# Scaling a head's exponentials on three engines instead of one, in a fused attention and mixture kernel

## The chip, the cores and the metric

The kernel runs on one core of one Trainium2 chip. The time is that of one execution on the device, in microseconds (us). Engines are called as the profile calls them: PE is TensorE (matmuls; PEld its weight loads), DVE is VectorE, ACT is ScalarE, POOL is GpSimd, SP is SyncE.

## What is computed

Causal attention with a decay for 4 batches of 8 heads, 576 tokens of 64 values, and on its output a mixture of four experts:

```python
scores = scale * np.matmul(q, k.transpose(0, 1, 3, 2))
log_f = np.log(np.clip(f, 0.0001, 1.0))
cum = np.cumsum(log_f, axis=-1)
decay = cum[:, :, :, None] - cum[:, :, None, :]
scores = np.where(causal, -1000000000.0, scores + decay)
scores = scores - np.max(scores, axis=-1, keepdims=True)
attn = np.exp(scores)
attn = attn / (np.sum(attn, axis=-1, keepdims=True) + 1e-09)
x = np.matmul(attn, v)          # heads side by side: 2304 x 512

p = domain_probs / (domain_probs.sum(-1, keepdims=True) + 1e-09)
for e in range(E):              # E = 4, w1[e] 512 x 1024, w2[e] 1024 x 512
    h = np.maximum(x @ w1[e], 0.0)
    out += p[:, e:e + 1] * (h @ w2[e])
```

The change touches the division of the exponentials by their sum.

## The kernel before

All is float32. A factor of a matmul is split into a high part (a Copy on ACT that rounds) and a low part (a subtraction of the high part), and a product is made of two or three matmuls of such parts.

Attention runs head by head. A batch is cut into two halves of query rows: half 0 has 256 queries in two tiles (t = 0 and 1), half 1 has 320 in three (t = 2, 3 and 4, with 384, 512 and 576 keys). A head of half 1 is called a long head here; there are 32, of which the 24 of batches 1 to 3 are "early", which means that their exponentials are divided before the product with `v`; in the others the product is scaled afterwards. For each tile of a head `qk_pe` (L378) makes the scores `s` in PSUM, `qk_min` (L392, DVE) adds the mask, keeps the negated scores in the SBUF tile `p` and their minimum in `nm`, and `qk_exp` (L407, ACT) turns `p` into exponentials in place and keeps their sum. When all tiles of an early head are done, `norm` adds 1e-9 to the sums (L435, DVE), takes the reciprocal `rs` (L438, DVE) and multiplies each tile of `p` by its column of `rs` (L442): on POOL for a long head, on DVE for a short one. One head later `tr_pe` (L479) transposes the blocks of `p` on PE, `tr_hi` (L489, ACT) and `tr_lo` (L496 and L504, DVE) turn them into `pth` and `ptl`, and `av_pe` (L529) multiplies them with `v` into `o`; `av_top` (L552, ACT) and `av_add` (L565, DVE) take that out of PSUM. Six buffers hold `p`, three of them for each long head.

Before a head is due, `prep` splits its queries and keys: `hi` (L325, ACT), `q` (L326, POOL), `kl` (L334) and the low half of `hi` (L340), the last two on DVE for a long head; `prep_v` does so for `v` (L306, ACT, and L313, DVE).

In between run the steps of the experts, 256 tokens and 256 hidden columns at a time: `l1` (L783), the gate, which makes `gh` (L794, ACT) and `gl` (L795, DVE), `l2` (L813), and the accumulation `acc` (L835, DVE). Their weights come by DMA, are rounded on ACT (`wh`, L750) and split on POOL (`wl`, L755; some of the first on DVE). A third part, after the attention, makes the last tokens' products with fewer matmuls (L953 and L1011); its sums and splits are on POOL too (L895, L910, L933).

The Python order of the attention's steps among the experts' steps follows fixed costs (`head_steps`, `pace`). Within it a planner with a simulated timeline chooses the order of the instructions on each engine; only the start-up (`startup`) has an order written out by hand. PE, ACT, DVE and POOL then each run their own queue in order, held by semaphores. DMAs are issued from SP.

Of the kernel before, what the change touches and what calls it, by code (L numbers as in the profile page):

```python
# [10 lines left out]
AF = mybir.ActivationFunctionType  # L11
ALU = mybir.AluOpType
# [57 lines left out]
def fused(ctx: ExitStack, tc: tile.TileContext, qk, v, f, probs, w, out):  # L70
    nc = tc.nc
# [182 lines left out]
    class Job:  # L254
# [178 lines left out]
        def norm(self, hh):  # L433
            rs = self.rs[:, hh, :]
            nc.vector.tensor_scalar(  # L435
                out=rs, in0=self.ssum[:, hh, :], scalar1=1e-9, scalar2=None, op0=ALU.add
            )
            nc.vector.reciprocal(out=rs, in_=rs)  # L438
            for t in self.its:
                i, x = t - self.its[0], self.p[hh, t][:, : TOK0[t] + 128]  # L440
                eng = nc.gpsimd if self.half else nc.vector
                eng.tensor_scalar(  # L442
                    out=x, in0=x, scalar1=rs[:, i : i + 1], scalar2=None, op0=ALU.mult
                )

        def spread(self):

# [815 lines left out]
```

## Time and profile before

| | us |
|---|---|
| three runs | 975.55, 976.8, 977.25; median 976.8 |
| the profiled execution, whole | 975.0 |
| its span, first to last instruction | 973.2 |

| engine | busy us | share of the span |
|---|---|---|
| PE | 960.6 | 99% |
| DVE | 676.4 | 70% |
| POOL | 513.6 | 53% |
| ACT | 467.2 | 48% |

Busy time is the time in which an engine has an instruction of its own under way; the ends of matmuls are modelled. The list of waits names, for each engine and line, who ended its idle time. The chain that ended last is followed back from the last instruction. The timeline shows each instruction with its start and duration, and several of one kind in a row as one piece.

### The profile page before, as it was taken

The page shows a single profiled execution, that of the slowest core. Times are in us where ns is not written, and L with a number is a line of the kernel's source. Part 1 is how long each engine was busy: PE and PEld are TensorE (multiplying, and loading weights), DVE is VectorE, ACT ScalarE, POOL GpSimd, SP SyncE. Part 2 cuts the span into 40 slices and gives each one's busy share as a digit, 9 for nine tenths or more (in the row PEclk, how much of TensorE's full clock was granted, in tenths as well). Part 3 has the DMA queues.
Part 4 walks back from the last instruction along what each step waited for, and adds up shares of the span by engine and source line. Part 5 has one row for each costly group of instructions (what it writes and reads, how often), then busy time and mean ns, then how long its engine had stood idle before and what let it go on. Part 6 is the DMA issues. An engine that isn't in the chain of part 4 may idle for free.

```text
span 973.2 us, 15567 instructions
## 1 busy us (share of the span) xinstructions
PE 960.6 (99%) x5638; PEld 843.7 (87%) x5638; DVE 676.4 (70%) x1413; ACT 467.2 (48%) x979; POOL 513.6 (53%) x511
## 2 busy tenths in 40 slices
PE   8999999999999999999999999999999999999998
PEld 6898999899899999998999998988788888888886
DVE  6877777877877676778769656357766666566665
ACT  7776664646656455556455544334323232233220
POOL 4988763502306547548457565778654444555410
PEclk9999999999999999999999999999999999999999
DMA  7765431322312312313313030421211112111002
GB/s 257 254 205 169 140 92 42 110 84 95 128 53 89 103 52 96 97 52 117 96 57 134 2 109 22 130 90 63 87 44 43 44 44 73 58 44 43 23 1 87
DMA packets 29822, 85.89 MB, mean 88 GB/s; under 512 B 3160, under 2 KB 5264, under 8 KB 29744
## 3 DMA queue, kind: packets, MB, share of 16 engines
q1 hardware_dynamic: 29744, 84.89, 26.8%
q8 instruction: 45, 0.74, 0.3%
q14 instruction: 33, 0.27, 0.1%
HBM read 80.00 MB, written 4.87 MB: 87 GB/s over the span
## 4 chain that ended last, share of the span: by engine, by line
PE 83%; POOL 5%; DVE 5%; issue 3%; DMA 2%; ACT 1%; SPq 0%; POOLq 0%; DVEq 0%; ACTq 0%
PE l L783 19%; PE l L813 19%; PE y L1011 17%; PE m L953 13%; PE s L378 5%; PE t L479 5%; PE o L529 5%; POOL bwl L933 2%; DMA wr<-in_w 2%; POOL wt L910 1%; POOL wl L755 1%; DVE v L313 1%; DVE kl L334 1%; POOL rx L895 1%; DVE rl L897 1%
## 5 line engine op out<-in xcount | busy, mean ns | idle before, releaser
L783 PE MATMUL l<-xl,wh 128*128 128x256 f32 x640 | 180.8, 283 | 0.3 <-DVE xl L673 0.3
L783 PE MATMUL l<-xh,wh 128*128 128x256 f32 x640 | 180.9, 283 | 0.2 <-ACT xh L672 0.2
L783 PE MATMUL l<-xh,wl 128*128 128x256 f32 x640 | 180.6, 283 | 0.0
L755 POOL TENSOR_TENSOR wl<-wr,wh 128x512 fp32r<-128x512 f32 x114 | 151.9, 1358 | 30.5 <-ACT wh L750 19.2
L835 DVE SCALAR_TENSOR_TENSOR acc<-y,prob,acc 128x512 f32<-128x512 f32 x120 | 88.3, 747 | 68.5 <-PE y L1011 68.5
L442 POOL TENSOR_SCALAR p<-p,rs 128x384 f32<-128x384 f32 (+2 forms) x72 | 107.8, 1513 | 50.1 <-DVE rs L438 46.8
L813 PE MATMUL l<-wh,gh 128*128 128x512 f32 x320 | 127.2, 397 | 0.8 <-DVE acc L835 0.8
L813 PE MATMUL l<-wl,gh 128*128 128x512 f32 x320 | 126.7, 396 | 0.0
L813 PE MATMUL l<-wh,gl 128*128 128x512 f32 x320 | 125.0, 394 | 0.0
L407 ACT ACTIVATE p<-p,nm 128x576 f32<-128x576 f32 (+2 forms) x160 | 95.6, 598 | 58.4 <-DVE nm L392 57.1
L783 PEld LDWEIGHTS l<-xl,wh 128*128 128x128 f32 x640 | 120.5, 188 | 3.3 <-DVE xl L673 0.5
L783 PEld LDWEIGHTS l<-xh,wh 128*128 128x128 f32 x640 | 120.4, 188 | 3.4 <-ACT xh L672 0.4
L933 POOL TENSOR_TENSOR bwl<-wr,bwh 128x256 fp32r<-128x256 f32 (+1 forms) x80 | 78.5, 1008 | 80.0 <-ACT bwh L930 80.0
L783 PEld LDWEIGHTS l<-xh,wl 128*128 128x128 f32 x640 | 120.4, 188 | 0.2
L392 DVE CUSTOM_DVE_ANT_0 p<-s,mask 128x288 f32<-128x288 f32 (+2 forms) x160 | 74.8, 478 | 57.6 <-PE s L378 52.4
L326 POOL CAST q<-raw 64x320 fp32r<-64x320 f32 (+1 forms) x56 | 27.3, 488 | 145.7 <-PE s L378 131.8
L1011 PE MATMUL y<-bwh,hh 128*128 128x512 f32 x256 | 101.2, 395 | 0.8 <-DVE acc L835 0.8
L1011 PE MATMUL y<-bwl,hh 128*128 128x512 f32 x256 | 101.1, 395 | 0.0
L1011 PE MATMUL y<-bwh,hl 128*128 128x512 f32 x256 | 100.4, 395 | 0.0
L953 PE MATMUL m<-rl,bwh 128*128 128x512 f32 x224 | 87.5, 390 | 0.0
L953 PE MATMUL m<-rh,bwh 128*128 128x512 f32 x224 | 87.4, 390 | 0.0
L953 PE MATMUL m<-rh,bwl 128*128 128x512 f32 x224 | 87.0, 392 | 0.0
(121 smaller groups left out, 2097.4 us busy)
## 6 DMA issues: line engine op xcount, KB each, us to landing
wr<-in_w SPq DMA_DIRECT2D x96, 512.0 KB
raw<-in_qk SPq DMA_DIRECT2D x16, 896.0 KB
raw<-in_qk SPq DMA_DIRECT2D x12, 512.0 KB
vr<-in_v SPq DMA_DIRECT2D x16, 320.0 KB
out<-acc SPq DMA_DIRECT2D x16, 256.0 KB
vr<-in_v SPq DMA_DIRECT2D x8, 128.0 KB
first<-in_qk SPq DMA_DIRECT2D x3, 256.0 KB
first<-in_v SPq DMA_DIRECT2D x4, 128.0 KB
```

Source lines behind the costliest of these rows:

```text
L378: nc.tensor.matmul(out=ps[:, at : at + z - a], lhsT=lhsT, rhs=rhs, start=(m == 0), stop=(m == 1),)
L392: nc.vector.tensor_tensor_reduce(out=pt[:, a:z], in0=ps, in1=mask[:, m0 + a : m0 + z], scale=-0.125, scalar=BIG if n == 0 else nm[:, col : ...
L407: return nc.scalar.activation(out=pt[:, :w_], in_=pt[:, :w_], func=AF.Exp, scale=-1.0, bias=self.nmax[hh][:, c : c + 1], accum_out=self.ss ...
L442: eng.tensor_scalar(out=x, in0=x, scalar1=rs[:, i : i + 1], scalar2=None, op0=ALU.mult)
L479: nc.tensor.transpose(ps[:, at : at + 128], self.p[hh, it][:, TOK0[jt] : TOK0[jt] + 128], ident)
L755: eng.tensor_tensor(out=wl[n][:, a:z], in0=wraw[n][:, a:z], in1=wh[n][:, a:z].bitcast(F32), op=ALU.subtract)
L783: nc.tensor.matmul(out=self.l1p[:, fi, :], lhsT=lhsT, rhs=rhs[:, k, :], start=(k == 0 and m == 0), stop=(k == 3 and m == 2),)
L813: nc.tensor.matmul(out=l2[tt], lhsT=lhsT, rhs=rhs, start=(self.ps == 0 and fi == 0 and m == 0), stop=(self.ps == 1 and fi == 1 and m == 2),)
L835: nc.vector.scalar_tensor_tensor(out=acc[c][:, tt, :], in0=ps, scalar=sc, in1=acc[c][:, tt, :], op0=ALU.mult, op1=ALU.add,)
L933: nc.gpsimd.tensor_tensor(out=lo[:, a:z], in0=x[:, a:z], in1=hi[:, a:z].bitcast(F32), op=ALU.subtract)
L953: nc.tensor.matmul(out=ps, lhsT=lhsT[:, o], rhs=rhs[:, k, :], start=(k == 0 and i == 0), stop=(k == 1 and i == 2),)
L1011: nc.tensor.matmul(out=ps, lhsT=lhsT, rhs=rhs, start=(fi == 0 and m == 0), stop=(fi == 1 and m == 2),)
```

## The change

For a long head, tile t = 2 (384 columns) is now scaled by an activation Copy on ACT whose scale is the column of `rs`, tile t = 3 (512 columns) on DVE, and tile t = 4 (576 columns) still on POOL. The short heads' tiles (t = 0 and 1) stay on DVE.

```diff
             for t in self.its:
                 i, x = t - self.its[0], self.p[hh, t][:, : TOK0[t] + 128]
-                eng = nc.gpsimd if self.half else nc.vector
-                eng.tensor_scalar(
-                    out=x, in0=x, scalar1=rs[:, i : i + 1], scalar2=None, op0=ALU.mult
-                )
+                r = rs[:, i : i + 1]
+                if t == 2:
+                    nc.scalar.activation(out=x, in_=x, func=AF.Copy, scale=r)
+                    continue
+                eng = nc.gpsimd if t == 4 else nc.vector
+                eng.tensor_scalar(out=x, in0=x, scalar1=r, scalar2=None, op0=ALU.mult)
```

## Rows read from the trace of the kernel before

**Rows 1.** Busy time by stretch, 290 to 576 us; columns in its first line.

```profile
core 0: us, PE busy (x) PEld busy (x) DVE busy (x) ACT busy (x) POOL busy (x), PEclk, DMA share, GB/s
290.00:576.00 286.00, 285.74 (x1932) 264.25 (x1931) 206.67 (x510) 160.05 (x332) 171.87 (x135) 1.00 0.25 84
```

**Rows 2.** Waits of PE and PEld, 290 to 580: total us, times, longest.

```profile
PE l L813 <- DVE acc L835: 0.3, 1, 0.3
...
PEld o L529 <- DVE ptl L496: 0.8, 3, 0.4
```

**Rows 3.** The page's chain that ended last: by engine, by line.

```profile
PE 83%; POOL 5%; DVE 5%; issue 3%; DMA 2%; ACT 1%; SPq 0%; POOLq 0%; DVEq 0%; ACTq 0%
PE l L783 19%; PE l L813 19%; PE y L1011 17%; PE m L953 13%; PE s L378 5%; PE t L479 5%; PE o L529 5%; POOL bwl L933 2%; DMA wr<-in_w 2%; POOL wt L910 1%; POOL wl L755 1%; DVE v L313 1%; DVE kl L334 1%; POOL rx L895 1%; DVE rl L897 1%
```

**Rows 4.** Timeline of PE: start, duration, what; in brackets idle time and releaser.

```profile
453.20 0.50 PE L813 MATMUL l<-wh,gh 128*128 128x512 f32 x1 [0.26 <-DVE acc L835]
...
596.51 0.50 PE L813 MATMUL l<-wh,gh 128*128 128x512 f32 x1 [0.56 <-DVE acc L835]
...
684.83 0.50 PE L1011 MATMUL y<-bwh,hh 128*128 128x512 f32 x1 [0.77 <-DVE acc L835]
```

**Rows 5.** Groups of L442 by shape, 290 to 580: count, busy us, mean ns.

```profile
L442 POOL TENSOR_SCALAR p<-p,rs 128x576 f32<-128x576 f32 x24 | 41.4, 1724 | 0.0
L442 POOL TENSOR_SCALAR p<-p,rs 128x512 f32<-128x512 f32 x24 | 37.6, 1565 | 0.0
...
L442 POOL TENSOR_SCALAR p<-p,rs 128x384 f32<-128x384 f32 x24 | 30.0, 1249 | 50.1 <-DVE rs L438 46.8 <-ACT pth L489 3.2
```

**Rows 6.** Timeline of POOL and PE, the head at 320 us.

```profile
320.82 4.48 POOL L442 TENSOR_SCALAR p<-p,rs 128x384 f32<-128x384 f32 x3
...
325.61 0.27 PE L479 MATMUL t<-ident,p 128*128 128x128 f32 x1
```

**Rows 7.** Groups of ACT by shape, whole span.

```profile
L591 ACT ACTIVATE xh<-xs 128x256 fp32r<-128x256 f32 x16 | 6.6, 414 | 9.7 <-DVE xs L581 9.7
L896 ACT ACTIVATE rh<-rx 128x512 fp32r<-128x512 f32 x8 | 4.9, 624 | 4.5 <-POOL rx L895 4.5
```

**Rows 8.** Line L442 on DVE, all: least, median, longest ns.

```profile
L442 DVE TENSOR_SCALAR p<-p,rs x32: 271/343/853, 93.0 to 197.1; 128x128 f32<-128x128 f32 x16, 128x256 f32<-128x256 f32 x16
```

**Rows 9.** Timeline of DVE, two short heads' pairs of scalings.

```profile
101.27 0.55 DVE L442 TENSOR_SCALAR p<-p,rs 128x128 f32<-128x128 f32 x2
...
119.02 1.12 DVE L442 TENSOR_SCALAR p<-p,rs 128x128 f32<-128x128 f32 x2
```

**Rows 10.** Timelines of DVE and POOL, at 315, 449 and 488 us.

```profile
314.58 0.74 DVE L334 TENSOR_TENSOR kl<-raw,hi 64x576 fp32r<-64x576 f32 x1
...
315.40 5.44 POOL L755 TENSOR_TENSOR wl<-wr,wh 128x512 fp32r<-128x512 f32 x4 [1.31 <-ACT wh L750]
...
317.12 1.15 DVE L435 TENSOR_SCALAR rs<-ss 128x3 f32<-128x3 f32 x1
...
448.71 2.53 POOL L755 TENSOR_TENSOR wl<-wr,wh 128x512 fp32r<-128x512 f32 x2
...
448.93 2.92 DVE L334 TENSOR_TENSOR kl<-raw,hi 64x576 fp32r<-64x576 f32 x1
...
487.61 0.17 DVE L435 TENSOR_SCALAR rs<-ss 128x3 f32<-128x3 f32 x1
```

**Rows 11.** Timelines of DVE and PE, the heads at 440 and 381 us.

```profile
439.45 0.49 DVE L496 TENSOR_TENSOR ptl<-t,pth 128x320 fp32r<-128x320 f32 x1
...
441.19 0.31 PE L529 MATMUL o<-ptl,v 128*128 128x320 f32 x1
...
381.98 0.49 DVE L496 TENSOR_TENSOR ptl<-t,pth 128x320 fp32r<-128x320 f32 x1
...
382.52 0.41 PE L529 MATMUL o<-ptl,v 128*128 128x320 f32 x1
```

**Rows 12.** Timelines of ACT and DVE, the head at 377 us.

```profile
377.03 0.19 ACT L407 ACTIVATION_READ_ACCUMULATOR p<-p,nm 128x1 f32 x1
...
381.15 0.16 DVE L438 RECIPROCAL rs<-rs 128x3 f32<-128x3 f32 x1
```

## The prediction

> **What bounds the kernel now.** I read the busy time by stage first, then who made TensorE wait, then the chain that ended last, and only then the operations that the change moves. The long heads that the change touches (three query tiles, half 1, batches 1 to 3: 24 heads) run from 290 to 576 us. In this stretch PE is busy for 285.74 of 286.00 us at the full granted clock, 1.00, which is the 2.4 GHz level [rows 1]. Everything else has room: DVE 206.67 us (72%), ACT 160.05 (56%), POOL 171.87 (60%). The list of waits says the same from the other side: in the whole stretch PE's matmuls waited once, 0.3 us, for an accumulation on DVE, and the weight loads 0.8 us in three pieces for `ptl` [rows 2]. The chain that ended last is 83% PE; POOL has 5% of it [rows 3], and the POOL lines that the page names there are the splits and sums of the late stage, not the scalings at L442. So a microsecond taken from POOL in this stretch is not a microsecond of the kernel. What the edit can do to the time is what it does to PE's waits, which are nearly nil.
>
> **How much can be gained at most.** PE's idle gaps from 290 us on, up to its last matmul, are 0.26 us at 453.20, 0.56 at 596.51 and 0.77 at 684.83 [rows 4], 1.59 us in all. A better order cannot take away more than these, and 1.59 us is 0.16% of 976.8. About 0.2%, 1.95 us, is what a measurement of this kernel can tell from no change. I leave the first 290 us out of account: there the heads have two query tiles, and the edit keeps those scalings on DVE.
>
> **The change part by part.** *Removed from POOL:* 24 scalings of 128x384 (30.0 us) and 24 of 128x512 (37.6 us); the 24 of 128x576 (41.4 us) stay [rows 5]. POOL in the stretch goes from 171.87 to 171.87 - 67.6 = 104.3 us, 36%. The three scalings of a head are one run of 4.49 us today; one alone takes 1.72. The last scaled tile is therefore ready some 2.7 us sooner. Who waits for it? The transposes of that head. In the tightest head the POOL run ends at 320.82 + 4.48 = 325.30 and the first transpose starts at 325.61 [rows 6], 0.3 us later; the other 23 have 0.8 to 9 us. No row shows PE waiting for POOL, so the 2.7 us go into slack that exists already: worth 0.
>
> *Added to ACT:* 24 Copies of 128x384, SBUF to SBUF, with a scale from a column. The trace of before has no such instruction at this width. A Copy of 128x256 takes 0.414 us and one of 128x512 0.624 [rows 7]; these are the bounds, and half-way between the widths lies half-way between the times, 0.52. 24 x 0.52 = 12.5 us, ACT goes to 172.5 us, 60%. Copy already runs on ACT in every head beside Exp, and the only table loads of the trace stand at lines 156 and 180 in the start, so none is added. A cost below nothing is excluded: it is work that ACT did not have.
>
> *Added to DVE:* 24 scalings of 128x512. The nearest rows are the same line on DVE in the short heads: a pair of 128x128 and 128x256, 384 columns in two instructions, takes 0.55 us when nothing holds it and 1.12 when something does [rows 9]. One instruction has one fixed start instead of two, so 512 columns lie between 0.34 (the median of all 32 of that line [rows 8]) and 0.55 x 512 / 384 = 0.73; I take 0.5. 24 x 0.5 = 12 us, and DVE goes to 218.7 us, 76%.
>
> What may be added on DVE is waiting for POOL. Undisturbed, the subtraction `kl` takes 0.74 us; begun 0.22 us after two of POOL's splits it took 2.92, and `rs`, one tiny instruction with a single tensor, took 1.15 while POOL split, where 0.17 is usual [rows 10]. Both have SBUF inputs alone. So the moved scaling can be held too, by about 1 us in a typical case (1.15 - 0.17), which makes 1.5 us the upper price of one and 36 us of DVE the upper sum (85% busy). On the other hand POOL's long runs at L442, which hold DVE in their turn, become 2.7 us shorter per head, and the splits behind them may start sooner. I take no net change in the holding and keep both ends for the range.
>
> The Trainium skill speaks against this edit here: "SBUF — State Buffer", section "SBUF: two separate sides", says that VectorE and GpSimd share a port pair which one instruction holds until it is done, for a VectorE operation with two SBUF inputs or in a two-port mode. This trace agrees in kind (2.92 us against 0.74), and even shows a wait over two GpSimd instructions in a row. [...]
>
> *Waits that the change adds.* All three scalings wait for `rs`. On DVE that is the instruction's own engine; queued behind it are the `ptl` subtractions of the head before, and the `o` matmuls wait for those. Their cover is the thinnest of the kernel: usually about a microsecond or more (last `ptl` ends at 439.94, first matmul that reads one starts at 441.19), but 0.05 us in the head at 381 (ends at 382.47, read at 382.52) [rows 11]; three of the 24 heads have under 0.7 us at their last `o` matmuls. An unheld 0.5 us there costs at most 3 x 0.5 = 1.5 us, and nothing where the planner puts it behind them. On ACT, what queues behind the new Copy are `pth` evictions, gates (`gh`) and the next head's exponentials. `rs` ends 0.6 to 3 us after the last exponential in 21 heads and 3.8 to 4.1 in three, of which the worst has 377.22 to 381.31 [rows 12]. Gates have more cover: in the whole stretch PE waits for no `gl` [rows 2]. No DMA is issued by any of the moved instructions, and SP's queue is not touched. The order on each engine comes from the planner, which sees other durations now, so PE's order may be shuffled too; at 100% busy with several microseconds between producer and reader, that has no sign that I can give.
>
> **The sum.** Gain 0 from POOL (at most 1.59 us through other waits), loss 0 to 1.5 us from DVE in front of `ptl`, 0 from ACT. The middle of the loss, about 0.7, against a chance that the wait at 453.20 goes, 0.3, leaves +0.4. The profiled execution took 975.0 us with a span of 973.2; the three timed runs have a median of 976.8, so I add the same sum to that: 977.2, hence a forecast of no measurable change.
>
> **Rivals.** *Slower, DVE held in front of `ptl`.* The mechanism is the wait on POOL above: the moved scaling, released by `rs`, meets POOL's 128x576 scaling, released by the same `rs`, or a split. It decides from the point where 1.5 us of delay exceed the cover of `ptl`. With today's order that is three heads, 3 x 1.2 = 3.6 us: 976.8 + 3.6 = 980.4. For it: three heads are already late for this very reason (`kl` held by splits), and the one wait of a PE matmul in the stretch came out of such a pile [rows 4, 10]. Against it: the scaling follows `rs` on the same engine and POOL needs a hand-over, so DVE should start first and POOL, which has the room, would wait. This rival is what the page of the Trainium skill named above leads one to expect.
>
> *Slower, ACT held.* If the Copy stands in ACT's queue ahead of the `pth` evictions, these start up to 4.1 + 0.5 us late, some 2.5 us more than the usual distance from `pth` to `o`. In the three heads where `rs` is that late: 3 x 2.5 = 7.5, 984.3 us. Against it: those evictions are ready before `rs` is, and the planner queues by readiness.
>
> *Faster.* POOL, relieved, starts its splits sooner, they no longer fall on `kl`, and the DVE piles behind PE's waits vanish: at most 1.59 us, 975.2, which is still inside 0.2%. Only if matmuls also follow each other more closely would it be more, say 974.7.
>
> *The edit does less than it says.* Only `t == 2` and `t == 4` leave DVE, and both occur in long heads alone, so it does what it says; this would end at no change as well.
>
> **How the numbers follow.** No measurable change 0.76 (977.2, from 975.2 to 978.7); DVE held 0.13 (980.4); ACT held 0.04 (984.3); faster 0.07 (974.7). That gives faster 0.07, same 0.76, slower 0.17. The range reaches from 974.6, which takes in the gain, to 980.8, which takes in the DVE rival with 0.4 us to spare; left out are the ACT rival and what lies beyond the worked-out price of the DVE rival.
>
> **What would show it.** In the changed profile: 24 ACT Copies of about 0.52 us, 24 DVE scalings of about 0.5 us (a mean above 0.8 means they are held), 24 POOL scalings of 1.7 us or somewhat more, POOL some 67 us lighter between 290 and 576. PE idle in that stretch should stay under 2 us. I am wrong if PE waits for `ptl` or `pth` in many heads, if PE's idle time outside the stretch changes by microseconds because the planner reorders the late stage, or if the time falls by more than PE's 1.59 us of idle.

## The result, and the profile after

| | kernel before | changed kernel |
|---|---|---|
| median of 4 runs each, side by side, us | 976.95 (975.55 to 977.25) | 982.2 (980.92 to 984.01) |
| ratio, 95% interval | 1 | 1.0055 [1.0037, 1.0073] |
| the profiled execution, us | 975.0 | 982.76 |
| its span, us | 973.2 | 980.9 |

The change makes the kernel slower: by 5.25 us between the medians, and by a ratio of 1.0055, whose interval lies clear of 1. A second set of runs (below, "changed again") gave 1.0047. The forecast was no measurable change, 977.2 us with a range to 980.8, and the measured time lies above that range.

The engines' busy times, from the page of the changed kernel, say that the exchange took place: POOL went from 513.6 to 449.4 us. PE went from 960.6 to 966.5, though it has the same matmuls to do.

```profile
PE 966.5 (99%) x5638; PEld 851.0 (87%) x5638; DVE 691.2 (70%) x1437; ACT 480.2 (49%) x1003; POOL 449.4 (46%) x463
```

The moved scalings themselves, as groups by shape from 290 to 580 us in the changed kernel (count, busy us, mean ns, then idle time before them and who ended it). They answer to [rows 5]: lines 443 and 446 are what line 442 was.

```profile
L446 POOL TENSOR_SCALAR p<-p,rs 128x576 f32<-128x576 f32 x24 | 44.4, 1849 | 79.5 <-DVE rs L438 60.5 <-ACT pth L491 19.1
...
L443 ACT ACTIVATE p<-p,rs 128x384 f32<-128x384 f32 x24 | 14.8, 618 | 17.2 <-DVE rs L438 17.2
...
L446 DVE TENSOR_SCALAR p<-p,rs 128x512 f32<-128x512 f32 x24 | 12.5, 521 | 0.1
```

All three are where the edit puts them, 24 each. Now the stretches, in the busy-time view of the changed kernel (columns in its first line; [rows 1] is the same view of before).

```profile
core 0: us, PE busy (x) PEld busy (x) DVE busy (x) ACT busy (x) POOL busy (x), PEclk, DMA share, GB/s
290.00:574.00 284.00, 284.00 (x1932) 263.92 (x1931) 223.81 (x548) 179.14 (x370) 105.14 (x85) 1.00 0.26 82
574.00:584.00 10.00, 5.83 (x18) 4.29 (x17) 8.66 (x9) 1.14 (x3) 9.23 (x7) 0.67 0.35 113
...
584.00:980.90 396.90, 391.25 (x1812) 322.79 (x1811) 238.49 (x332) 115.59 (x198) 186.47 (x193) 1.00 0.18 56
...
577.50:584.30 6.80, 5.01 (x13) 4.09 (x14) 5.19 (x6) 0.00 (x0) 6.03 (x5) 0.50 0.49 157
```

Where the moved instructions run, among the long heads, PE has not one wait left: 284.00 of 284.00 us. In the ten microseconds after them it is busy for 5.83, and its clock is at 0.50, the 1.2 GHz level, for some 7 us (577.5 to 584.3). The PE timeline of the changed kernel (start, duration, what; in brackets idle time and who ended it) shows the same place; it answers to [rows 4].

```profile
574.13 0.28 PE L785 MATMUL l<-xh,wl 128*128 128x256 f32 x1
576.16 0.47 PE L815 MATMUL l<-wh,gh 128*128 128x512 f32 x1 [1.75 <-DVE acc L837]
...
579.29 0.80 PE L815 MATMUL l<-wh,gh 128*128 128x512 f32 x1 [2.42 <-DVE acc L837]
...
580.30 0.63 PE L815 MATMUL l<-wh,gl 128*128 128x512 f32 x1
580.73 0.63 PE L815 MATMUL l<-wh,gh 128*128 128x512 f32 x1
...
584.35 0.28 PE L785 MATMUL l<-xh,wh 128*128 128x256 f32 x1
...
642.04 0.39 PE L815 MATMUL l<-wh,gl 128*128 128x512 f32 x1
642.27 0.39 PE L955 MATMUL m<-rh,bwh 128*128 128x512 f32 x1
...
692.61 0.50 PE L1013 MATMUL y<-bwh,hh 128*128 128x512 f32 x1 [1.40 <-DVE acc L837]
```

PE waits 1.75 us and then 2.42 us for an accumulation `acc` on DVE. Behind the second wait its matmuls of 512 columns follow each other at 0.43 us (580.30 to 580.73) where later ones do at 0.23 (642.04 to 642.27). Why `acc` is late stands in DVE's and POOL's timelines of the same microseconds. DVE first.

```profile
568.55 6.68 DVE L899 TENSOR_TENSOR rl<-xf,rh 128x512 fp32r<-128x512 f32 x4 [0.82 <-ACT rh L898]
575.26 0.75 DVE L837 SCALAR_TENSOR_TENSOR acc<-l,prob,acc 128x512 f32<-128x512 f32 x1
575.93 2.64 DVE L899 TENSOR_TENSOR rl<-xf,rh 128x512 fp32r<-128x512 f32 x2
578.49 0.74 DVE L837 SCALAR_TENSOR_TENSOR acc<-l,prob,acc 128x512 f32<-128x512 f32 x1
```

POOL in the changed kernel, beside it:

```profile
565.76 5.51 POOL L757 TENSOR_TENSOR wl<-wr,wh 128x512 fp32r<-128x512 f32 x4 [11.04 <-ACT wh L752]
571.23 1.76 POOL L897 TENSOR_TENSOR rx<-xf,xf 128x512 f32<-128x512 f32 x1
573.07 1.61 POOL L897 TENSOR_TENSOR rx<-xf,rx 128x512 f32<-128x512 f32 x1
574.64 6.30 POOL L757 TENSOR_TENSOR wl<-wr,wh 128x512 fp32r<-128x512 f32 x4
```

The `rl` subtractions are the low parts of the last tokens' inputs, the first work of the third part. Four of them stand ahead of the first `acc` in DVE's queue, and POOL splits weights and makes sums from 565.76 on without a pause. The four take 6.68 us, 1.67 each, beside splits and sums alike. The same place in the kernel before, DVE and then POOL:

```profile
589.65 3.56 DVE L897 TENSOR_TENSOR rl<-xf,rh 128x512 fp32r<-128x512 f32 x3 [0.82 <-ACT rh L896]
593.24 0.75 DVE L835 SCALAR_TENSOR_TENSOR acc<-l,prob,acc 128x512 f32<-128x512 f32 x1
593.91 1.88 DVE L897 TENSOR_TENSOR rl<-xf,rh 128x512 fp32r<-128x512 f32 x3
...
596.97 1.28 DVE L897 TENSOR_TENSOR rl<-rx,rh 128x512 fp32r<-128x512 f32 x2
```

```profile
589.05 1.30 POOL L895 TENSOR_TENSOR rx<-xf,xf 128x512 f32<-128x512 f32 x1 [13.58 <-ACT tmp L552]
590.42 1.64 POOL L895 TENSOR_TENSOR rx<-xf,rx 128x512 f32<-128x512 f32 x1
597.80 1.62 POOL L895 TENSOR_TENSOR rx<-rx,xf 128x512 f32<-128x512 f32 x1 [5.74 <-DVE rl L897]
```

There, three `rl` and not four precede the first `acc`; POOL has no split, only two sums, and where it is idle an `rl` takes 0.63 to 0.64 us (1.88 / 3 and 1.28 / 2). PE waited 0.56 us at that place [rows 4].

Why did this block of work meet POOL's splits? It came sooner. Both timelines of ACT, before and after, have as a landmark the last eviction of the attention, which opens the third part:

```profile
587.80 0.43 ACT L552 ACTIVATE tmp<-o 64x320 f32<-64x320 f32 x1 [3.99 <-PE o L529]
```

```profile
566.70 0.43 ACT L554 ACTIVATE tmp<-o 64x320 f32<-64x320 f32 x1
```

It is 21 us earlier. The planner works with the durations of the new scalings, by which a head's scaling is over sooner, and its order brings the attention's last heads forward among the experts' steps: ahead of the attention's last matmul PE does 150 of the experts' matmuls fewer than before. PE's own work does not get shorter by that, it is only done in another order. The first `rl` moves with it, from 589.65 to 568.55, to where POOL has eight splits to do.

**The tally of the two profiled executions.** PE's last matmul starts at 968.50 before and at 976.25 after, 7.75 us later.

| place | us later there |
|---|---|
| first `l1` matmul, 25.10 and 26.54 | 1.4 |
| from there to 290 us | 1.2 |
| from 290 us to the first `m` matmul, 635.13 and 642.27 | 4.6 |
| the wait of `y` at 692.61, 1.40 for 0.77 | 0.6 |

The third line is a balance. PE's waits are 4.17 us instead of 0.26 + 0.56, which makes 3.35, but idle time is not the whole of it. An estimate from the two traces, with each matmul put at its usual spacing in the kernel before, shows where PE falls behind. Up to 573 us the changed kernel *gains* 1.2 us, 0.9 of it at the place of the old wait at 453.20. From 573 to 585 us it loses 7.0. The kernel before then loses 1.0 at its own wait at 596.51, and 0.2 in small pieces. Of the 7.0 us, 4.17 are the two waits and some 2.2 the lower clock: from 579.29 on, ten matmuls of 512 columns and three of 256 take 5.06 us, to 584.35, and behind the wait of the kernel before the same thirteen take 2.90, from 596.51 to the start of this one:

```profile
599.41 0.28 PE L783 MATMUL l<-xh,wh 128*128 128x256 f32 x1
```

The first two lines of the table I put down to the execution and not to the change. In the start both kernels do the same, but eight matmuls that took 1.67 us in one profiled execution took 2.84 in the other, and the kernel before with an edit far behind that place shows the late start as well (first `l1` at 26.56 in e9 below). The 1.2 us arise around 100 us, where the granted clock from 95 to 120 us was 1.00 before and 0.93 after. It was 0.93 in the kernel before with an edit far behind that place (e6), too, and 1.00 in the second profile of the changed kernel (e10). Without these two lines 5.2 us are left, which is what the medians differ by.

### The profile page after: what moved, and what is told of

The parts are those of the page before. It is cut to its first block, busy times and chain, and to the rows that moved or that the text cites. A ratio compares the mean times of both kernels' runs of the same rounds, so it can differ in the third digit from the quotient of the medians.

```text
span 980.9 us, 15535 instructions
## 1 busy us (share of the span) xinstructions
PE 966.5 (99%) x5638; PEld 851.0 (87%) x5638; DVE 691.2 (70%) x1437; ACT 480.2 (49%) x1003; POOL 449.4 (46%) x463
## 5 line engine op out<-in xcount | busy, mean ns | idle before, releaser
L797 DVE SCALAR_TENSOR_TENSOR gl<-l,gh 128x512 fp32r<-128x512 f32 x80 | 54.8, 685 | 47.2 <-ACT gh L796 46.9
```

The source lines that it names most:

```text
L797: nc.vector.scalar_tensor_tensor(out=self.gl, in0=self.l1p, scalar=0.0, in1=self.gh.bitcast(F32), op0=ALU.max, op1=ALU.subtract,)
```

## Experiments

Two theories were open after the traces. *Order:* the third part's first pieces now lie beside POOL's splits, DVE is held there, `acc` is late. *Moved work:* the scalings on ACT or DVE cost something that the profile does not show as a wait. All kernels were run beside the kernel before; ratios are to that one, with 95% intervals.

**e1 and e2, each half of the change alone.** The first has tile 2 on ACT and leaves 3 and 4 on POOL:

```diff
-                eng = nc.gpsimd if t == 4 else nc.vector
+                eng = nc.gpsimd if self.half else nc.vector
```

> Half of the change: tile 2 on ACT, tiles 3 and 4 on POOL as before. Theory A (the shorter scaling lets the planner end the attention some 20 us sooner, so that the subtractions `rl` of the late stage's inputs stand in DVE's queue ahead of `acc` just when POOL splits weights, and PE waits for `acc`, then runs at the lower clock for some microseconds): the order at that place is the same here, so PE waits 3 to 5 us for `acc` near 575 us and the time is 981 to 983 us. Rival B (the scaling moved to DVE delays `ptl`): DVE has none here, so 976 to 978. Rival C (ACT is held for `rs`): 980 to 983, with PE's waits on `pth` or `gh` among the heads and not at 575.

The second has tile 3 on DVE and leaves 2 and 4 on POOL:

```diff
-                if t == 2:
-                    nc.scalar.activation(out=x, in_=x, func=AF.Copy, scale=r)
-                    continue
-                eng = nc.gpsimd if t == 4 else nc.vector
+                eng = nc.gpsimd if t in (2, 4) else nc.vector
```

> The other half: tile 3 on DVE, tiles 2 and 4 on POOL. Theory A: same order at the end of the attention, PE waits 3 to 5 us for `acc` near 575 us, 981 to 983. Rival B: 980 to 983, with PE's waits on `ptl` among the heads. Rival C: 976 to 978.

Measured: e1 981.83 us, 1.0055 [1.0035, 1.0075]; e2 981.27 us, 1.0051 [1.0032, 1.007]. PE's timeline of e1 and then of e2:

```profile
574.51 0.47 PE L815 MATMUL l<-wh,gh 128*128 128x512 f32 x1 [1.44 <-DVE acc L837]
...
577.58 0.79 PE L815 MATMUL l<-wh,gl 128*128 128x512 f32 x1 [2.37 <-DVE gl L797]
```

```profile
577.40 0.47 PE L812 MATMUL l<-wh,gh 128*128 128x512 f32 x1 [1.48 <-DVE acc L834]
...
580.53 0.79 PE L812 MATMUL l<-wh,gh 128*128 128x512 f32 x1 [2.42 <-DVE acc L834]
```

Each half alone costs the whole 0.5%, in the same place and in waits of nearly the same length; the second wait of e1 is for `gl`, which stands in the same queue of DVE. A cost of the moved work would have been split between them. What both have in common is that a head's scaling is shorter, and in both the attention ends early: its last eviction starts at 565.04 in e1 and at 568.22 in e2, where it started at 587.80 before.

**e3 and e5, the low parts off DVE.** If `rl` in front of `acc` is the cause, the changed kernel with these subtractions on POOL must lose the waits. e3 is the changed kernel, e5 the kernel before, both with

```diff
-        nc.vector.tensor_tensor(out=lo, in0=x, in1=hi.bitcast(F32), op=ALU.subtract)
+        nc.gpsimd.tensor_tensor(out=lo, in0=x, in1=hi.bitcast(F32), op=ALU.subtract)
```

> The changed kernel, but the 14 subtractions `rl` of the late stage's inputs on POOL in place of DVE. Theory A: `acc` no longer stands behind them, PE waits under 1 us at the end of the attention, the clock stays up there, and the time falls to 976.5 to 978.5. Rivals B and C: nothing among the heads is touched, so 981 to 983. Against A also if POOL, which now has some 18 us more work there, makes PE wait for `wl`.

> The kernel before (all three scalings on POOL) with the 14 subtractions `rl` on POOL, to tell what the three engines themselves are worth once the end of the attention is repaired. If the split over three engines is worth nothing by itself, this kernel lies within 1.5 us of the same edit on the changed kernel (975.3): 974.5 to 976.5, and PE's wait of 0.56 us for `acc` near 596 us is gone. If relieving POOL is worth something of its own, it lies at 977 or more.

Measured: e3 975.31 us, 0.9985 [0.9972, 0.9998]; e5 976.95 us, 1.0004 [0.999, 1.0017]. Busy times of e3 over the boundary:

```profile
560.00:600.00 40.00, 40.00 (x262) 36.53 (x261) 9.82 (x15) 17.60 (x28) 36.17 (x29) 1.00 0.21 66
```

PE has no wait and the clock stays at 1.00. The attention ends as early as in the changed kernel (last eviction at 564.16), so ending early costs nothing by itself. The same edit is worth 0.7% to the changed kernel (1.0055 to 0.9985) and nothing to the one before. That control is not a clean one: e5 came out between its two expectations, and while its wait near 596 us is gone, PE has two new ones, which e3 has not:

```profile
632.10 0.50 PE L813 MATMUL l<-wh,gh 128*128 128x512 f32 x1 [0.69 <-ACT gh L794]
636.73 0.50 PE L953 MATMUL m<-rh,bwh 128*128 128x512 f32 x1 [1.61 <-ACT bwh L930]
```

**e4 and e6, the pieces queued later.** In the changed kernel (e4) and in the one before (e6), the goal for the end of the attention and of the third part's input pieces lies 5 steps before the last and not 10, and the pieces issued after the attention's last stage are tied behind what the engines had been given until then:

```diff
-AHEAD = 10
+AHEAD = 5
...
+    def queued():
+        stack = ExitStack()
+        for e in (mybir.EngineType.Activation, mybir.EngineType.DVE, mybir.EngineType.Pool):
+            last = next(i for i in reversed(nc.cur_bb.bb.instructions) if i.engine == e)
+            stack.enter_context(tc.issue_after(last))
+        return stack
...
-            with behind() if at < stage_end[FIRST] else ExitStack():
+            with behind() if at < stage_end[FIRST] else queued() if at >= stage_end[-1] else ExitStack():
```

> The changed kernel with its three engines, but the goal by which attention and the late stage's inputs must be traced is 5 steps before the end in place of 10, and these input pieces queue behind what is traced before them, so that one or two `rl` stand between two `acc` and no split of weights between the first five sums. Theory A: PE waits under 1 us at the end of the attention and the time is 976.5 to 978.5. Rivals B and C: 981 to 983.

> The kernel before with the goal of 5 steps and the input pieces queued behind what is traced before them. Here the attention ends late by itself, so the pieces come some microseconds after those of the changed kernel with this edit. If the three engines are worth nothing by themselves: 974.5 to 977, within 1.5 us of 975.2. If they help only through the order at the end: the same. If relieving POOL is worth something of its own: over 977.

Measured: e4 975.24 us, 0.9987 [0.9975, 0.9999]; e6 976.08 us, 0.9992 [0.998, 1.0004]. DVE's timeline of e4:

```profile
581.39 1.19 DVE L899 TENSOR_TENSOR rl<-xf,rh 128x512 fp32r<-128x512 f32 x1
582.50 0.74 DVE L837 SCALAR_TENSOR_TENSOR acc<-l,prob,acc 128x512 f32<-128x512 f32 x1
583.16 1.72 DVE L899 TENSOR_TENSOR rl<-xf,rh 128x512 fp32r<-128x512 f32 x2
```

Here the engines' loads are untouched: `rl` is on DVE and the splits on POOL as in the changed kernel. One `rl` instead of four is ahead of the first `acc`, no split is beside it, and the loss is gone. The edit also moves the attention's end back, to 579.48 for the last eviction, so it takes away part of the shift itself.

**e7 and e9, the splits off POOL.** The other side of the collision: the weight splits of four late steps go from POOL to DVE, in the changed kernel (e7) and in the one before (e9).

```diff
-W_DVE = tuple(range(2, 16, 2))
+W_DVE = tuple(range(2, 16, 2)) + (54, 55, 56, 57)
```

> The changed kernel with the four weight blocks that POOL splits beside the `rl` subtractions (blocks 54 to 57) split on DVE. POOL then has only its sums at that place. If what holds DVE is POOL's splits, an `rl` takes about 0.7 us where it took 1.67, PE waits under 1 us for `acc` there although DVE has 8 instructions of some 0.7 us more to do, and the time is 976 to 978.5. If DVE was late merely because it has too much to do there, the wait stays at 3 us or more and the time at 981 or more.

> The kernel before (three scalings on POOL) with weight blocks 54 to 57 split on DVE, the control of the changed kernel with this edit (975.2). If the three engines are worth nothing by themselves: 974 to 976.7. If relieving POOL is worth something once the end is repaired: 976.7 or more.

Measured: e7 975.17 us, 0.9979 [0.9965, 0.9993], the lowest ratio of all, though its interval overlaps those of e3 and e4; e9 977.9 us, 1.0005 [0.9989, 1.0022]. DVE's timeline of e7:

```profile
571.38 0.72 DVE L899 TENSOR_TENSOR rl<-xf,rh 128x512 fp32r<-128x512 f32 x1
...
575.00 1.88 DVE L899 TENSOR_TENSOR rl<-xf,rh 128x512 fp32r<-128x512 f32 x3
```

DVE has more to do and is faster at it: 0.72 and 0.63 us for an `rl` that took 1.67 beside splits and sums. The attention ends early here, too (567.92), and PE has no wait at the boundary. The order is another one as well (one `rl` ahead of the first `acc`), so this pair does not separate the hold from the place in the queue. The edit does not mend the kernel before: e9 still waits there, 0.84 us for 0.56, and its 977.9 us lie on the side of the expectation where relieving POOL is worth something, though the kernel before, run beside it, took 977.01.

**e8, a shorter scaling with nothing moved.** The kernel before, with tiles 2 and 3 of the 24 long heads left unscaled:

```diff
             for t in self.its:
                 i, x = t - self.its[0], self.p[hh, t][:, : TOK0[t] + 128]
+                if t in (2, 3):
+                    continue
                 eng = nc.gpsimd if self.half else nc.vector
```

> The kernel before with the scalings of tiles 2 and 3 of the long heads left out (only tile 4 is scaled, on POOL): POOL is relieved as in the changed kernel, and neither ACT nor DVE gets anything. If the slowdown comes from the order that the planner makes when the scaling is short, PE waits 2.5 us or more for `acc` (or `gl`) near 575 us and the time is 979.5 to 983. If it comes from the work moved to ACT and DVE, the time is 976 to 977.5 and no such wait is there.

Measured: 979.87 us, 1.0027 [1.0011, 1.0042]. Who made PE wait in e8 from 290 to 600 us (total us, times, longest), and then DVE's timeline:

```profile
PE l L815 <- DVE acc L837: 2.4, 1, 2.4
PE l L815 <- DVE gl L797: 0.7, 1, 0.7
```

```profile
569.54 7.88 DVE L899 TENSOR_TENSOR rl<-xf,rh 128x512 fp32r<-128x512 f32 x5 [1.04 <-ACT rh L898]
577.46 0.75 DVE L837 SCALAR_TENSOR_TENSOR acc<-l,prob,acc 128x512 f32<-128x512 f32 x1
```

This kernel has 48 instructions fewer than the one before, none on another engine, and it is slower all the same, by 0.27%, through the same wait: five `rl` in front of `acc`, 1.58 us each. Its attention ends at 567.48 (last eviction), so the shorter scaling alone moves that end. About half of the loss, then, needs no moved work at all (0.27% against 0.47% and 0.55%). That it is smaller than in the changed kernel goes with its shorter waits, 3.1 us for 4.17, and with a shorter time at the lower clock, 3.4 us for 6.8.

**The changed kernel again**, on the chip of e9:

> The changed kernel itself, in five rounds beside the one above. Theory A: 980.5 to 983 in every round, with PE's waits of 3 to 5 us for `acc` near 575 us and the lower clock behind them. If the slowdown were only the scatter of the clock in the first 110 us, some of its runs would lie at 977 or less.

Measured: 981.42 us, 1.0047 [1.0031, 1.0062]. The runs reach from 979.2 to 983.68 us, a little beyond the expectation on both sides, and none lies near 977. PE's two waits at the boundary are as they were:

```profile
574.82 0.47 PE L815 MATMUL l<-wh,gh 128*128 128x512 f32 x1 [1.73 <-DVE acc L837]
577.95 0.80 PE L815 MATMUL l<-wh,gh 128*128 128x512 f32 x1 [2.43 <-DVE acc L837]
```

**Together.** The theory of the moved work falls: with the boundary mended in three different ways, the kernel with the change stands at 0.9985, 0.9987 and 0.9979, and the kernel before with the same three edits at 1.0004, 0.9992 and 1.0005. All three mended kernels also came out about 1 us faster than the least that was expected of them.

What the change is worth by itself stays roughly known. The pairs say 0.05% (0.9987 / 0.9992) to 0.26% (0.9979 / 1.0005), at intervals of 0.12 to 0.17% on each number, so the least of them is not told from nothing; and the two larger ones use the controls e5 and e9, in which PE has waits that the mended kernels have not. The traces show one gain: PE's wait near 453 us is there in all four with the old scaling (before, e5, e6 and e9: 0.25 to 0.26 us) and in none of the eight others, and it cost some 0.9 us (the estimate above).

What stays open is how the loss divides between the hold, DVE's longer instructions beside POOL's, and the queue, the number of `rl` ahead of `acc`. By the rows, four unheld `rl` would have taken 4 x 0.64 = 2.6 us, `acc` would have ended near 572 us, and PE, which had work until 574.4, would not have waited; so the hold looks decisive for the first wait. But no run kept the order and took the hold away, since every move of an instruction changes the planner's order.

## Why the prediction was wrong

**The bound, and where the gain is not.** Right in the main. POOL's 66.7 us (171.87 of 286 us to 105.14 of 284) were worth about 1 us of PE's time, and among the long heads the time was PE's before and after. The most that could be gained was worked out too low, for it counted idle time alone: at the wait of 0.26 us some 0.9 us were lost.

**The moved work.** Nearly right in size and right in effect. DVE's scaling took 521 ns in the mean where 0.5 us had been taken; half of them took no more than 479 ns, and the longest 750. It was not held as the first rival feared, although POOL's scaling of 128x576 is released by the same `rs`: that one became slower instead, 1849 ns for 1724. ACT's Copy was mis-sized: 618 ns for 0.52 us. Its row of 128x512 at 0.624 [rows 7] has a constant scale, and half-way between widths left out that the scale from a column may cost something of its own; 24 x 0.1 us are 2.4 us of ACT, which PE never felt.

**The cover of `ptl`.** The loss of 0 to 1.5 us did not come: PE and its weight loads have no wait for `ptl` between 290 and 580 us in the changed kernel, where [rows 2] had three. The gap at 453.20 went, too, for which the sum had set 0.3 us against the loss.

**The rivals.** *ACT held* did not happen: ACT waited for `rs` 19 times, 17.2 us in all, and no wait of PE came of it. *DVE held by POOL* had the right mechanism, DVE queued behind POOL until a matmul is late, and the wrong place and consumer: not the new scaling in front of `ptl`, but the old `rl` in front of `acc`, 20 us after the last instruction that the change touches. Its price of 3.6 us for three short covers was worked out from the heads and is not the 3.35 us of waits at the boundary; that the two lie near each other is chance. The page that was weighed there, the Trainium skill's "SBUF — State Buffer", section "SBUF: two separate sides", agrees in kind with the held `rl`: a VectorE operation with two SBUF inputs is locked out by a GpSimd one (0.64 against 1.67 us). POOL did not go free either: beside `rl` a split took up to 1.58 us in the mean of a run of four, for 1.26. The section speaks of the time of one instruction; `kl` took 3.15 us at 450.42 in the changed kernel beside two splits of 1.27 us each, so here the wait outlasts one of them.

**The step that failed** is the last sentence on the waits that the change adds: the planner's shuffle "at 100% busy with several microseconds between producer and reader, that has no sign that I can give". From "no sign" the sum took zero, and the covers had been looked up only where the change issues instructions. Two things in the rows spoke for a sign. The planner orders by durations, so taking 2.7 us from each long head's chain could move the attention's end by far more than that, 21 us as it came out, and with it all that starts when the attention ends. And that end had no cover: of PE's three gaps after 290 us the one at 596.51, 0.56 us for `acc` [rows 4], lies right there, with three `rl` queued ahead of it. A gap that exists is a cover of zero; what delays the producer there is paid in full. What the runs showed in place of that zero is 4.17 us of waits for two `acc`, the first queued behind four `rl` of 1.67 us each, the second behind two more. POOL's idle 13.58 us ahead of its first sum, in the kernel before, was the room that kept DVE free there, and a reader of it could have asked what would fill it. The list of what would make the prediction wrong did name this case, without a place or a price.

**The clock.** A second term was missing from the sum: a wait of PE can cost more than its length. Of the 7.0 us lost between 573 and 585 us, some 2.2 are the stretch at the 1.2 GHz level that began in the second wait (5.06 us for 2.90).

## What to carry to other kernels

Where a planner orders the queues, making an idle engine's work shorter is no local edit: ask what will now start sooner, which queues it joins, and whether the work there still fits beside its new neighbours. Look up the existing gaps of the bound engine over the whole span first, wherever the edit lies, for a place without cover is where a shuffle is paid. And when a change costs more than its instructions can explain, run each half alone, and run it with the work left out: if both halves and the omission lose time in the same wait, it is the order, and a repair of the order bounds what the change is worth.

## What the runs showed of the chip

- In the second of two waits of 1.75 and 2.42 us, with 0.7 us of work between them, PE's granted clock fell from 1.00 to 0.50, and it stayed there for some 7 us (577.5 to 584.3), most of which PE was working. In e8, with waits of 2.4 and 0.7 us, it was at 0.50 from 579.3 to 582.7. Behind the wait of 1.61 us in e5 it stayed at 1.00.
- One and the same subtraction of 128x512 took 0.63 us on DVE with POOL idle and, in the mean of a run, 1.32 to 1.67 beside POOL's splits and sums. The splits in turn went from 1.26 us (the run of four at 5.04 to 5.06) to 1.38 and 1.58 (5.51 and 6.30 for four). Both lose.
- An ACT Copy of 128x384 with its scale from a column took 618 ns, as long as one of 128x512 with a constant scale (624 [rows 7]).
- The kernel before spreads from 974.59 to 980.34 us over its runs. Over the twelve profiled executions of all the kernels some of such a spread arises in the first 30 us: the first `l1` starts at about 25.0 or from 26.4 us on, and the same eight matmuls at 4.8 us take 1.67 us before and 2.84 in the changed kernel.
